# An attention, gating and mixing kernel on one core: key loads sent two blocks ahead, a limit of one side operation per engine and tick, and a normalisation on VectorE

## The chip, the cores and the metric

The kernel runs on one core of one Trainium2 chip. The metric is the device time of one execution in microseconds (us); lower is better. A profile is one execution taken by the hardware profiler: it lists the instructions of TensorE (PE, with its weight loads PEld), VectorE (DVE), ScalarE (ACT), GpSimd (POOL) and the DMA queue of SyncE (SP), each with its start and duration.

## What is computed

```python
def _attn_ref(q, k, v, n_global, n_local):          # (2, 8, 768, 64); 8 global keys, window 96
    scores = scale * np.matmul(q, k.transpose(0, 1, 3, 2)) + bias    # bias: -slope * distance
    scores = np.where(keep, scores, -1000000000.0)  # keep: global keys, or 0 <= rel < n_local
    a = softmax(scores)
    return np.matmul(a, v)

def _moe_ref(x, w_in, w_spatial, b_spatial, w_out): # x (2, 768, 512)
    h = np.maximum(x @ w_in, 0.0)                   # (2, 768, 1024)
    u, v = h[..., :512], h[..., 512:]
    v_n = (v - mean(v)) / np.sqrt(var(v) + 1e-06)
    v_s = np.einsum('ts,bsd->btd', w_spatial, v_n) + b_spatial[None, :, None]
    return (u * v_s) @ w_out

def _moe2_ref(x, U, V, w_ch1, w_ch2):
    u = x + (x.transpose(0, 2, 1) @ U @ V).transpose(0, 2, 1)
    return u + np.maximum(u @ w_ch1, 0.0) @ w_ch2
```

The three run one after the other. Weights come as 64-bit floats and are decoded on the chip.

## The kernel before

**Attention** runs over 12 blocks g (2 batches of 6 blocks of 128 queries), 8 heads in 4 pairs r, with 232 keys in a block's window (128 in the first block of a batch). In round g the emitted order is: scores of block g (`em_s`, 16 matmuls from the buffer `raw`, two buffers in turn), values of block g-2 (`em_pv`), softmax of block g (`em_soft` on DVE, `em_exp` on ACT, `em_norm` on DVE and POOL), and the transposes of block g-1 (`em_t`, four steps r, each copied out of PSUM to `ptb` by ACT or DVE). An engine runs its instructions in the order in which they were emitted.

**Side work** is emitted between these. It is kept as chains of operations (`Plan.add`); `Plan.tick` (line 160) walks through the chains and emits each next operation whose planned start lies close to TensorE's planned time, and repeats the walk until nothing more fits. `Plan.flush` emits what is left of given chains, at the place where their result is needed. The planned times come from prices in the code (`price`, line 105).

The side work of the attention stage is: the decoding of the first layer's `v` weights (`early_work`, line 667: four chains `P["wv"]`, each one ACT `Abs`, four DVE operations on 128x512, an ACT rounding and a POOL subtraction; places `rawin`, `masks`, `stg`), flushed before the first first-layer step; the spatial weights (`P["ws"]`, three chains: one DMA of 768 KB into one half of `stg`, then three ACT roundings and three subtractions, on POOL or DVE) and the spatial bias `P["bs"]`, flushed before the first spatial step; and `ln` (line 737), the reciprocal square root of the normalisation for three token tiles, followed by `ln_apply` for each tile (DVE scaling, ACT rounding, POOL subtraction into `vn`).

**Fillers** are matmul steps of the later layers put between the transposes by `fill(more)`: first-layer steps (`s_m1_v`, in rounds 4 to 9, 24 steps of batch 0), then spatial steps (`s_m2`, 48 steps of batch 0, from round 10 on). The spatial step with s == 3 flushes the second `ln` group of its batch. After the attention come the first layer of batch 1 (72 matmuls into `work`), the `u` half with its gating (`m1_u`, 8 steps, using `win`), the spatial product of batch 1, and then the output and mixing layers. `ln` of batch 1 belongs to the stretch of `m1_u`.

DMAs go out in order on SP's queue: `o_load` (keys and queries of a block), `o_vals` (values), and the weights.

Of the kernel before, what the change touches and what calls it, by code (L numbers as in the profile page):

```python
# [65 lines left out]
class Plan:  # L66
# [3 lines left out]
    def __init__(self, nc):  # L70
# [4 lines left out]
            ((nc.vector, "V"), (nc.scalar, "A"), (nc.gpsimd, "G"), (nc.tensor, "T"), (nc.sync, "SP")))  # L75
        self.chains = []

    @staticmethod
    def size(ap):
        n = 1  # L80
        for x in ap.shape[1:]:
            n *= x
        return n
# [63 lines left out]
                held[key][which, cols] = end  # L147
        return True

    def add(self, ops, after=()):  # L150
        c = Chain(ops, after, self.calm)
        self.chains.append(c)
        return c

    def emit(self, c):
# [2 lines left out]
            self.chains.remove(c)  # L158

    def tick(self):  # L160
        now, more = self.free["T"], True
        while more:
            more = False
            for c in sorted(self.chains, key=lambda c: c.calm):
                key = c.ops[0][0]
                if any(d.ops for d in c.after) or self.free[key] > now + (CALM if c.calm else ROOM):
                    continue
                self.probing = 0.0
                c.ops[0][1]()
                start, self.probing = self.probing, None  # L170
                if start <= max(now, self.free[key]) + STALL:
                    self.emit(c)
                    more = True

# [13 lines left out]
def kernel(ctx: ExitStack, tc: tile.TileContext, qk, qt, kn, vab, vn_, gl_,  # L188
# [11 lines left out]
    def body(dense, sb, pp):  # L200
# [142 lines left out]
        if not dense:  # L343
# [148 lines left out]
            def attention():  # L492
                for e in range(2):
                    o_load(0, e)[0][1]()
                o_vals(0)[0][1]()
                A.activation(out=sm[:, 12:13], in_=nc.const_aps.tensor(0.0, (128, 1)), func=AF.Exp)
                V.memset(bank[4], 0.0)
                V.memset(bank[7], 0.0)
                masks_before()
                make_identity(nc, ident)  # L500
                loads = {}
                for e in range(2):
                    o_load(1, e)[0][1]()
                pvals = {0: []}
                early_work([t_x11[:, 0:1536], t_x11[:, 1536:3072], t_x10[:, 1536:3072], stg[:, 0:1536]])
                pvals[1] = [plan.add(o_vals(1))]
                masks_first()
                masks_second()
                masks_third()
                for h in range(5, 8):  # L510
                    bias_g(Bt, rel, mk, h)


                for g in range(NBL + 2):
                    more = 0 if g < 4 else 1 if g < TWO else 3
                    if g == NB:
                        second_x()
                    xs = None
                    if g < NBL:
                        flush(loads.get(g, []))  # L520
                        for r in range(NP):
                            em_s(g, r)
                        if 0 < g and g + 1 < NBL:
                            loads[g + 1] = [plan.add(o_load(g + 1, e)) for e in range(2)]
                        tick()
                    if g >= 2:
                        flush(pvals[g - 2])
                        em_pv(g - 2)
                        if g < NBL:
                            pvals[g] = [plan.add(o_vals(g))]  # L530
                        xs = em_x(g - 2)
                    if g < NBL:
                        if g == 0:
                            for h in range(2, 4):
                                o_bias(B0, d0, m1, h)[1]()
                        em_soft(g, 0)
                        em_exp(g, 0)
                    if 0 < g <= NBL:
                        em_norm(g - 1, 1)
                    if g < NBL:  # L540
                        em_soft(g, 1)
                        em_exp(g, 1)
                        if g == 0:
                            for h in range(4, 8):
                                o_bias(B0, d0, m1, h)[1]()
                    if xs:
                        xs[0]()
                    for r in range(NP):
                        if xs and r == 1:
                            xs[1]()  # L550
                        if 0 < g <= NBL:
                            em_t(g - 1, r)
                            tick()
                        fill(more)
                        if g < NBL:
                            if r < 2:
                                em_soft(g, 2 + r)
                                em_exp(g, 2 + r)
                            if r == 1:
                                em_norm(g, 0)  # L560
                        tick()
                    if g == 0:
                        for h in range(5):
                            o_bias(Bt, rel, mk, h)[1]()
                        plan.add([("V", f) for f in o_counts() + o_flag()])
                    if 2 <= g < NB + 2:
                        fillers.extend(s_m1_v(0, g - 2, 6))
                    if g == TWO - 1:
                        fillers.extend(s_m2(0, 6))

# [96 lines left out]
        def early_work(places):  # L667
# [12 lines left out]
            u_ = tl(T_UT, N_UT, "u")  # L680
            P["ut"] = u_.rearrange("p (k t) -> p k t", k=KB)
            P["vw"] = [[u_[:, DM * n:DM * n + DM] for n in range(NB)]]
            P["bs"] = plan.add([o_dma(bsp, b_sp.partition_broadcast(128))], P["wv"][-1:])

            def make(t, c):
                return ([o_dma(t, w_sp.rearrange("p s t -> p (s t)")[:, c:c + 1536])]
# [49 lines left out]

        def ln(b, g):

            c = slice(3 * g, 3 * g + 3)
            e, q_, r = ve[:, b, c], rt[:, b, c], rs[:, b, c]  # L740

            def o_mult(o_, i0, i1):
                return "G", lambda: G.tensor_tensor(out=o_, in0=i0, in1=i1, op=ALU.mult)

            newton = [o_mult(q_, r, r), o_mult(q_, q_, e),
                      ("G", lambda: G.tensor_scalar(out=q_, in0=q_, scalar1=-0.5, scalar2=1.5, op0=ALU.mult, op1=ALU.add)),
                      o_mult(r, r, q_)]
            first = plan.add([
                ("V", lambda: V.tensor_scalar(out=e, in0=mv[:, b, c, 1], scalar1=1.0e-6, scalar2=None, op0=ALU.add)),
                ("V", lambda: V.tensor_scalar(out=r.bitcast(I32), in0=e.bitcast(I32), scalar1=1, scalar2=-1,  # L750
                                              op0=ALU.logical_shift_right, op1=ALU.bitwise_xor)),
                ("G", lambda: G.tensor_scalar(out=r, in0=r, scalar1=-1.8346686e-20, scalar2=0.0, op0=ALU.mult,
                                              op1=ALU.add))] + 3 * newton)
            return [plan.add(ln_apply(b, t), [first]) for t in range(3 * g, 3 * g + 3)]

        def ln_apply(b, t):
            vw = P["vw"][b][t]
            hi, lo = (P["vn"][b][l][:, t] for l in range(2))
            return [("V", lambda: V.tensor_scalar(out=vw, in0=vw, scalar1=mv[:, b, t, 0:1], scalar2=rs[:, b, t:t + 1],
                                                  op0=ALU.subtract, op1=ALU.mult)),  # L760
                    o_rnd(A, hi, vw), o_sub(G, lo, vw, hi)]

        def m1_u(b, f, j, bk):
            for k in range(KB):
# [273 lines left out]
```

## Time and profile before

| | us |
|---|---|
| median of 3 runs | 548.46 (546.75 to 548.96) |
| profiled execution, device time | 549.51 |
| its span, first to last instruction | 547.7 |
| PE busy | 513.8 |
| DVE / ACT / POOL busy | 299.7 / 212.0 / 196.6 |

All computing instructions carry line 56 (a recording helper), so groups are told apart by the names of what they write and read. Mean granted TensorE clock is 0.973 of full speed. PE is without a gap in most of the span; where it has gaps, the releaser beside an idle time names the instruction that came last before PE went on. A granted clock below 1 in a stretch is a share of the stretch in which TensorE ran at the lower of its two levels (1.2 GHz instead of 2.4).

### The profile page before, as it was taken

The numbers are of one execution on the slowest core, as the hardware profiler recorded it, in microseconds if no ns is written. First come the engines' busy times: TensorE is split into PE (matmuls) and PEld (weight loads), VectorE is DVE, ScalarE is ACT, GpSimd is POOL, SyncE is SP. The second block draws the span as 40 slices with busy tenths as digits, with TensorE's granted clock in tenths as the row PEclk, the third lists the DMA queues.
The fourth block names the chain that finished last, engine by engine and source line by source line (L and its number), as shares of the span: only waits on it lengthen the run. The fifth ranks groups of instructions, "written<-read, shape, count | busy, mean of one in ns | idle before, by whom it ended". The sixth has DMA issues, their size and how long they took to land.

```text
span 547.7 us, 7987 instructions
## 1 busy us (share of the span) xinstructions
PE 513.8 (94%) x2916; PEld 454.6 (83%) x2916; DVE 299.7 (55%) x702; ACT 212.0 (39%) x510; POOL 196.6 (36%) x265
## 2 busy tenths in 40 slices
PE   5579989699999899999999999999999999999994
PEld 3458868599989799888898989989989889899893
DVE  8886587343588963388699876866032011111113
ACT  4588768441244421355454234243122122221220
POOL 5466666621158801222024243232331332322310
PEclk9969989899999799999999999999999999999999
DMA  8617634130142110422204444240011000000003
GB/s 302 245 51 230 216 112 167 39 116 1 20 135 75 32 44 0 155 77 78 77 1 153 158 151 142 89 153 2 1 44 72 1 0 1 2 0 1 0 3 120
DMA packets 13521, 44.75 MB, mean 82 GB/s; under 512 B 1568, under 2 KB 3744, under 8 KB 11424
## 3 DMA queue, kind: packets, MB, share of 16 engines
q1 hardware_dynamic: 13328, 44.14, 23.1%
q8 instruction: 25, 0.41, 0.3%
q14 instruction: 24, 0.20, 0.1%
q10 hardware_dynamic: 144, 0.00, 0.0%
HBM read 40.99 MB, written 3.15 MB: 81 GB/s over the span
## 4 chain that ended last, share of the span: by engine, by line
PE 82%; DVE 7%; POOL 4%; ACT 4%; issue 2%; DMA 1%; ACTq 0%; POOLq 0%
PE bank L56 82%; DVE prob L56 2%; POOL sm L56 1%; ACT prob L56 1%; POOL vn L56 1%; DVE sm L56 1%; DVE y L56 1%; ACT ptb L56 1%; DVE stg L56 1%; DMA ni<-in_gl_dram 1%; DVE work L56 1%; DVE bias L56 1%; POOL wo L56 1%; POOL x L56 0%; DVE u L56 0%
## 5 line engine op out<-in xcount | busy, mean ns | idle before, releaser
L56 POOL TENSOR_TENSOR wch<-f,wch 128x512 fp32r<-128x512 f32 x64 | 86.1, 1366 | 213.3 <-ACT wch L56 213.3
L56 PE MATMUL bank<-wch,h 128*128 128x512 f32 x576 | 139.4, 396 | 0.0
L56 PE MATMUL bank<-x,wch 128*128 128x384 f32 x768 | 139.1, 337 | 0.0
L56 PEld LDWEIGHTS bank<-x,wch 128*128 128x128 f32 x768 | 134.5, 188 | 3.1
L56 PEld LDWEIGHTS bank<-wch,h 128*128 128x128 f32 x576 | 107.9, 188 | 23.2
L56 DVE SCALAR_TENSOR_TENSOR h<-bank,h 128x384 fp32r<-128x384 f32 x64 | 35.6, 556 | 141.5 <-ACT h L56 141.5
L56 ACT ACTIVATE h<-bank 128x384 fp32r<-128x384 f32 x64 | 31.4, 491 | 179.5 <-PE bank L56 179.5
L56 PE MATMUL bank<-wsp,vn 128*128 128x384 f32 x288 | 59.9, 362 | 7.0 <-POOL vn L56 5.0
L56 PEld LDWEIGHTS bank<-wsp,vn 128*128 128x128 f32 x288 | 53.0, 202 | 10.2 <-POOL vn L56 7.7
L56 POOL TENSOR_SCALAR prob<-prob,sm 128x232 f32<-128x232 f32 (+1 forms) x96 | 43.7, 473 | 40.8 <-DVE sm L56 19.8
L56 ACT ACTIVATE prob<-prob,sm 128x232 f32<-128x232 f32 (+1 forms) x96 | 44.4, 464 | 34.4 <-DVE sm L56 33.0
L56 DVE TENSOR_SCALAR f<-f 128x512 f32<-128x512 f32 (+1 forms) x64 | 41.4, 683 | 9.5 <-ACT f L56 9.3
L56 DVE SCALAR_TENSOR_TENSOR f<-raw,f 128x512 int32<-128x512 int32 x64 | 43.9, 726 | 0.1
L56 PE MATMUL bank<-win,x 128*128 128x512 f32 x144 | 40.1, 414 | 0.0
L56 PE MATMUL bank<-ident,prob 128*128 128x128 f32 (+1 forms) x176 | 29.6, 295 | 11.0 <-ACT ptb L56 10.9
L56 ACT ACTIVATE wch<-f 128x512 fp32r<-128x512 f32 x64 | 36.9, 625 | 1.0 <-DVE f L56 1.0
L56 PEld LDWEIGHTS bank<-ident,prob 128*128 128x128 f32 (+1 forms) x176 | 21.6, 144 | 18.6 <-POOL prob L56 10.5
L56 PE MATMUL bank<-x,win 128*128 128x384 f32 x192 | 34.2, 338 | 1.2 <-POOL win L56 0.7
L56 PE MATMUL bank<-wo,x 128*128 128x512 f32 x144 | 35.3, 395 | 0.0
L56 PEld LDWEIGHTS bank<-x,win 128*128 128x128 f32 x192 | 33.2, 188 | 2.0 <-POOL win L56 1.0
L56 PE MATMUL bank<-raw 64*128 64x232 f32 (+1 forms) x192 | 27.8, 436 | 7.5 <-DMA raw<-in_qk_dram 6.7
L56 PEld LDWEIGHTS bank<-raw 64*128 64x128 f32 x192 | 21.5, 238 | 12.8 <-DMA raw<-in_qk_dram 7.1
(85 smaller groups left out, 523.9 us busy)
## 6 DMA issues: line engine op xcount, KB each, us to landing
raw<-in_w_ch_dram SPq DMA_DIRECT2D x16, 1024.0 KB, 4.7
raw<-in_qk_dram SPq DMA_DIRECT2D x20, 360.0 KB, 4.8
vals<-in_vab_dram SPq DMA_DIRECT2D x10, 512.0 KB, 3.6
out_dram<-y SPq DMA_DIRECT2D x12, 256.0 KB, 2.2
stg<-in_w_in_dram SPq DMA_DIRECT2D x5, 512.0 KB, 5.0
stg<-in_w_sp_dram SPq DMA_DIRECT2D x3, 768.0 KB, 6.0
stg<-in_w_out_dram SPq DMA_DIRECT2D x4, 512.0 KB, 3.8
raw<-in_qk_dram SPq DMA_DIRECT2D x4, 256.0 KB, 5.0
```

The lines of the kernel that those rows point to most:

```text
L56: return f(*a, **kw)
```

## The change

- `o_load` for block g+2 is emitted directly after the scores of block g (before: as a chain for block g+1, added after the scores of block g and emitted by ticks). `o_vals` is emitted directly too. The `tick()` after the scores is gone.
- From the start of the attention to the end of round 11 a tick emits at most one side operation per engine (`plan.most = 1`).
- `ln` no longer uses POOL: for batch 0 the start value and three Newton steps of three operations run on DVE; for batch 1 an ACT `Sqrt`, a DVE `reciprocal` and one Newton step. Its chains and those of `ln_apply` are put in front of all others. The subtraction of the odd token tiles goes to DVE.
- The spatial bias waits until all four `v` weight chains are emitted, and the spatial chunk of the second staging half waits for it (before: that chunk could go at once).
- Round 10 runs one filler after each transpose instead of three, rounds from 11 on four.

```diff
-    def add(self, ops, after=()):
+    def add(self, ops, after=(), front=False):
         c = Chain(ops, after, self.calm)
-        self.chains.append(c)
+        self.chains.insert(0 if front else len(self.chains), c)
         return c
...
     def tick(self):
-        now, more = self.free["T"], True
+        now, more, count = self.free["T"], True, dict.fromkeys(LAG, 0)
...
+                if self.most and count[key] >= self.most:
+                    continue
                 self.probing = 0.0
                 c.ops[0][1]()
                 start, self.probing = self.probing, None
                 if start <= max(now, self.free[key]) + STALL:
+                    count[key] += 1
                     self.emit(c)
                     more = True
...
                 early_work([t_x11[:, 0:1536], t_x11[:, 1536:3072], t_x10[:, 1536:3072], stg[:, 0:1536]])
-                pvals[1] = [plan.add(o_vals(1))]
+                o_vals(1)[0][1]()
+                plan.most = 1
...
-                    more = 0 if g < 4 else 1 if g < TWO else 3
+                    more = 0 if g < 4 else 1 if g < TWO else 1 if g == TWO else 4
...
                     if g < NBL:
-                        flush(loads.get(g, []))
                         for r in range(NP):
                             em_s(g, r)
-                        if 0 < g and g + 1 < NBL:
-                            loads[g + 1] = [plan.add(o_load(g + 1, e)) for e in range(2)]
-                        tick()
+                        if g + 2 < NBL:
+                            for e in range(2):
+                                o_load(g + 2, e)[0][1]()
                     if g >= 2:
-                        flush(pvals[g - 2])
                         em_pv(g - 2)
                         if g < NBL:
-                            pvals[g] = [plan.add(o_vals(g))]
+                            o_vals(g)[0][1]()
                         xs = em_x(g - 2)
...
+                    if g == NBL - 1:
+                        plan.most = 0
...
-            P["bs"] = plan.add([o_dma(bsp, b_sp.partition_broadcast(128))], P["wv"][-1:])
+            P["bs"] = plan.add([o_dma(bsp, b_sp.partition_broadcast(128))], P["wv"])
+            user[1] = [P["bs"]]
...
-            newton = [o_mult(q_, r, r), o_mult(q_, q_, e),
-                      ("G", lambda: G.tensor_scalar(out=q_, in0=q_, scalar1=-0.5, scalar2=1.5, op0=ALU.mult, op1=ALU.add)),
-                      o_mult(r, r, q_)]
-            first = plan.add([
-                ("V", lambda: V.tensor_scalar(out=e, in0=mv[:, b, c, 1], scalar1=1.0e-6, scalar2=None, op0=ALU.add)),
-                ("V", lambda: V.tensor_scalar(out=r.bitcast(I32), in0=e.bitcast(I32), scalar1=1, scalar2=-1,
-                                              op0=ALU.logical_shift_right, op1=ALU.bitwise_xor)),
-                ("G", lambda: G.tensor_scalar(out=r, in0=r, scalar1=-1.8346686e-20, scalar2=0.0, op0=ALU.mult,
-                                              op1=ALU.add))] + 3 * newton)
-            return [plan.add(ln_apply(b, t), [first]) for t in range(3 * g, 3 * g + 3)]
+            newton = [stt(q_, r, -0.5, r, ALU.mult, ALU.mult),
+                      ("V", lambda: V.tensor_tensor(out=q_, in0=q_, in1=e, op=ALU.mult)),
+                      stt(r, q_, 1.5, r, ALU.add, ALU.mult)]
+            root = [("A", lambda: A.activation(out=q_, in_=e, func=AF.Sqrt)),
+                    ("V", lambda: V.reciprocal(out=r, in_=q_))]
+            bits = [o_ts(r.bitcast(I32), e.bitcast(I32), 1, -1, ALU.logical_shift_right, ALU.bitwise_xor),
+                    o_ts(r, r, -1.8346686e-20, None, ALU.mult)]
+            first = plan.add([o_ts(e, mv[:, b, c, 1], 1.0e-6, None, ALU.add)]
+                             + (root + newton if b else bits + 3 * newton), front=True)
+            return [plan.add(ln_apply(b, t), [first], True) for t in range(3 * g + 2, 3 * g - 1, -1)][::-1]
...
-                    o_rnd(A, hi, vw), o_sub(G, lo, vw, hi)]
+                    o_rnd(A, hi, vw), o_sub((G, V)[t % 2], lo, vw, hi)]
```

## Rows read from the trace of the kernel before

**Rows 1.** The page: PE's busy tenths and granted clock in 40 slices.
```profile
PE   5579989699999899999999999999999999999994
PEclk9969989899999799999999999999999999999999
```
**Rows 2.** Stretches: us, busy (instructions) of PE, PEld, DVE, ACT, POOL; clock; DMA share; GB/s.
```profile
17.00:45.00 28.00, 20.20 (x164) 16.28 (x165) 23.95 (x83) 18.91 (x58) 16.31 (x25) 0.82 0.39 139
70.00:79.00 9.00, 6.71 (x35) 4.69 (x35) 6.64 (x33) 5.60 (x20) 5.86 (x22) 0.81 0.37 142
100.00:113.00 13.00, 8.17 (x33) 6.40 (x33) 3.79 (x13) 3.20 (x8) 6.22 (x11) 0.74 0.00 1
160.00:174.00 14.00, 12.76 (x73) 12.12 (x72) 12.05 (x17) 4.95 (x9) 12.11 (x26) 1.00 0.26 75
181.00:190.00 9.00, 6.79 (x20) 5.35 (x20) 8.93 (x11) 4.55 (x9) 6.52 (x5) 0.64 0.12 34
```
**Rows 3.** PE in order of time: start us, us, what, count, [idle before <-releaser].
```profile
17.84 3.47 PE L56 MATMUL bank<-raw 64*128 64x232 f32 x16 [1.61 <-DMA raw<-in_qk_dram]
...
30.68 1.92 PE L56 MATMUL bank<-ident,prob 128*104 128x128 f32 x8 [6.47 <-ACT ptb L56]
...
40.92 1.84 PE L56 MATMUL bank<-raw 64*128 64x232 f32 x16
...
45.00 0.95 PE L56 MATMUL bank<-win,x 128*128 128x512 f32 x3
...
49.28 1.84 PE L56 MATMUL bank<-raw 64*128 64x232 f32 x16
...
106.72 3.14 PE L56 MATMUL bank<-wsp,vn 128*128 128x384 f32 x7 [3.75 <-POOL vn L56]
...
162.06 10.86 PE L56 MATMUL bank<-x,win 128*128 128x384 f32 x61 [0.66 <-POOL win L56]
...
183.74 25.27 PE L56 MATMUL bank<-wsp,vn 128*128 128x384 f32 x124 [1.25 <-POOL vn L56]
```
**Rows 4.** DVE in order of time, between the softmax of blocks 1 and 2.
```profile
17.73 0.99 DVE L56 TENSOR_SCALAR rawin<-rawin 128x512 f32<-128x512 f32 x2 [0.89 <-ACT rawin L56]
...
21.58 1.49 DVE L56 TENSOR_SCALAR masks<-masks 128x512 int32<-128x512 int32 x1
22.99 0.41 DVE L56 TENSOR_SCALAR stg<-stg 128x512 int32<-128x512 int32 x1
...
25.80 0.68 DVE L56 TENSOR_TENSOR wsp<-stg,wsp 128x512 fp32r<-128x512 f32 x1
...
27.07 0.39 DVE L56 CUSTOM_DVE_ANT_0 prob<-bank,bias 128x232 f32<-128x232 f32 x1
```
**Rows 5.** The SP queue's DMA issues in order of time.
```profile
6.17 0.51 SPq L56 DMA_DIRECT2D stg<-in_w_sp_dram  x1
...
7.61 4.91 SPq L56 DMA_DIRECT2D raw<-in_qk_dram  x4
...
59.92 0.33 SPq L56 DMA_DIRECT2D stg<-in_w_sp_dram  x1
```
**Rows 6.** ACT in order of time: the table load, and a spatial-weight rounding.
```profile
1.19 1.28 ACT L56 ACT_TABLE_LOAD   x1 [1.19 <-PEq L1025]
...
65.95 0.63 ACT L56 ACTIVATE wsp<-stg 128x512 fp32r<-128x512 f32 x1 [2.63 <-DMA stg<-in_w_sp_dram]
```
**Rows 7.** POOL in order of time, from 97 us on.
```profile
97.53 0.20 POOL L56 TENSOR_SCALAR sm<-sm 128x3 f32<-128x3 f32 x1
...
105.41 3.71 POOL L56 TENSOR_TENSOR vn<-u,vn 128x512 fp32r<-128x512 f32 x3
```
**Rows 8.** Groups by line, 150 to 195 us: count | busy us, mean ns | idle before.
```profile
L56 POOL TENSOR_TENSOR vn<-work,vn 128x512 fp32r<-128x512 f32 x6 | 8.6, 1468 | 0.0
...
L56 DVE TENSOR_SCALAR work<-work,sm 128x512 f32<-128x512 f32 x6 | 7.1, 1214 | 1.7 <-POOL sm L56 1.7
...
L56 DVE TENSOR_SCALAR sm<-sm 128x3 f32<-128x3 f32 (+1 forms) x4 | 1.4, 355 | 0.0
```

More of the change, by code (lines that the diff above doesn't have):

```diff
@@ L76, in __init__ @@
         self.chains = []
+        self.most = 0
     @staticmethod
@@ L500, in attention @@
                 make_identity(nc, ident)
-                loads = {}
                 for e in range(2):
                     o_load(1, e)[0][1]()
-                pvals = {0: []}
                 early_work([t_x11[:, 0:1536], t_x11[:, 1536:3072], t_x10[:, 1536:3072], stg[:, 0:1536]])
-                pvals[1] = [plan.add(o_vals(1))]
+                o_vals(1)[0][1]()
+                plan.most = 1
                 masks_first()
@@ L740, in ln, with stt, o_ts @@
             e, q_, r = ve[:, b, c], rt[:, b, c], rs[:, b, c]
-            def o_mult(o_, i0, i1):
-                return "G", lambda: G.tensor_tensor(out=o_, in0=i0, in1=i1, op=ALU.mult)
-            newton = [o_mult(q_, r, r), o_mult(q_, q_, e),
-                      ("G", lambda: G.tensor_scalar(out=q_, in0=q_, scalar1=-0.5, scalar2=1.5, op0=ALU.mult, op1=ALU.add)),
-                      o_mult(r, r, q_)]
-            first = plan.add([
-                ("V", lambda: V.tensor_scalar(out=e, in0=mv[:, b, c, 1], scalar1=1.0e-6, scalar2=None, op0=ALU.add)),
-                ("V", lambda: V.tensor_scalar(out=r.bitcast(I32), in0=e.bitcast(I32), scalar1=1, scalar2=-1,
-                                              op0=ALU.logical_shift_right, op1=ALU.bitwise_xor)),
-                ("G", lambda: G.tensor_scalar(out=r, in0=r, scalar1=-1.8346686e-20, scalar2=0.0, op0=ALU.mult,
-                                              op1=ALU.add))] + 3 * newton)
-            return [plan.add(ln_apply(b, t), [first]) for t in range(3 * g, 3 * g + 3)]
+            def stt(o_, i0, sc, i1, op0, op1):
+                return "V", lambda: V.scalar_tensor_tensor(out=o_, in0=i0, scalar=sc, in1=i1, op0=op0, op1=op1)
+            def o_ts(o_, i0, s1, s2, op0, op1=ALU.add):
+                return "V", lambda: V.tensor_scalar(out=o_, in0=i0, scalar1=s1, scalar2=s2, op0=op0,
+                                                    **({} if s2 is None else {"op1": op1}))
+            newton = [stt(q_, r, -0.5, r, ALU.mult, ALU.mult),
[8 more added lines that the diff above has]
+            return [plan.add(ln_apply(b, t), [first], True) for t in range(3 * g + 2, 3 * g - 1, -1)][::-1]
         def ln_apply(b, t):
```

## The prediction, made before the changed kernel was run

> **What bounds the kernel now.** I read first the page's slices: PE is nine tenths busy almost everywhere, and its holes and the lowered clock lie in the first 200 us of 548 [rows 1]. Only that part can change; from the third layer on PE runs without a hole until the last output. Second the table of stretches [rows 2], which I cut where PE has holes. In each, stretch minus PE busy is idle time, and (1 - clock) x stretch is what the lower clock (1.2 instead of 2.4 GHz) cost at most. Stage A, 17 to 45 us: 7.8 idle and 5.0 clock, 12.8. Stage B, 70 to 79: 2.3 and 1.7, 4.0. Stage C, 100 to 113: 4.8 and 3.4, 8.2. Stage D, 160 to 174 and 181 to 190: 1.2 + 2.2 idle and 3.2 clock, 6.7 with rounding. Together 31.7 us; apart from the start no edit can give more. Third, PE in order of time, which names who ended each hole [rows 3]: a key load (1.6 us before 17.84), a copy on ACT (6.5 before 30.68), the normalised tiles from POOL (3.75 before 106.72; 1.25 before 183.74). Fourth, the named engine's own order around each hole.
>
> **The change part by part.**
>
> *Stage A: key loads ahead, one side operation per tick, spatial chunk later.* Before the hole at 30.68 DVE ran one bulk of side work, from 17.73 until its softmax of block 2 began at 27.07: 9.3 us of decoding, small counts and one spatial subtraction [rows 4]. Softmax, ACT's exponentials and its copy stand behind this in order, so PE waited. With one operation per tick, and no tick behind the scores, the four chains' 16 DVE operations are spread over the ticks of rounds 2 and 3 (8 each). They stay in front of the same flush, so DVE's own work is not less. What does go: the spatial subtraction, 0.68 [rows 4], moves behind stage A with its ACT and POOL parts; and integer scalings that ran beside POOL's spatial subtractions took up to 1.49 against 0.41 without [rows 4]. Three stood there, at most 3.2 lost; I take 2.0. So DVE needs 23.95 - 2.7 = 21.3 us of a stage of 28.0 [rows 2], and the gain has 6.7 as its upper end. I take 4.5, leaving 2.2 of the 4.0 us that DVE idles there now, since softmax still waits for PE and ACT. The load of block 2 was issued behind a 768 KB spatial chunk (6.17, then 7.61 us, [rows 5]); that chunk now comes later and the load waits only for the scores of block 0. The 1.6 us before 17.84 go, but PE then meets the DVE bound, so they are not counted apart. The lower end is none gained, for the limit may leave operations over for the flush at the first filler (45.00, [rows 3]).
>
> The row of 1.49 against 0.41 is, by the Trainium skill (SBUF — State Buffer, Who interferes with whom), an exclusive lock of a port pair that VectorE and GpSimd share. By that rule the spatial chunk would carry its loss of 2.0 us into a later stage; there PE has fillers to run meanwhile, and the sum stays; without them it would be -13.0.
>
> *The direct loads add waits on SP*: a load for g+2 waits for the scores of block g, and values for the product of block g-2; behind them on SP stand the bias and the spatial chunks. Those are first used in round 10, and the last one was issued at 59.92 [rows 5], four rounds earlier, so I cost this at nothing; without that cover a chunk's 6.0 us from issue to use (59.92 to 65.95, [rows 5, 6]) would be bare.
>
> *Stage B.* Its hole of 2.3 us goes back to ACT: it stood 2.63 us at a spatial rounding whose DMA had not landed [rows 6], and the softmax of the next block stood behind. The change doesn't take this away: a rounding is still emitted when the plan believes the chunk there. Of two chunks issued late, one waited; now all three are late, and the limit lets only one rounding stand in a tick. Ends: -4.0 (no wait) and +4.0 (two waits of this price). I take 0, between them, since the one row speaks for either.
>
> *Stage C.* `ln` of tiles 3 to 5 ended the hole: its 13 small POOL operations began at 97.53, three DVE scalings and a softmax step followed, and POOL's three subtractions from 105.41 [rows 7]; PE went on at 106.72. After: 12 small DVE operations, which a DVE group on three elements puts at 0.36 [rows 8], at most 4.3 us, one per tick; the 16 ticks of round 10 hold them and the three scalings, and two of the subtractions go to DVE. Above all round 10 runs only 4 of the 12 spatial steps, so the first step that needs tile 3 falls in round 11, a round later: 8.4 us, as from 40.92 to 49.28 [rows 3]. All 8.2 us are the upper end; none is the lower. I take 6.0: small operations 4.3, scalings 3 x 0.41 and subtractions 2 x 0.68 [rows 4] put up to 6.9 us in front of round 10's softmax, where fewer fillers cover it, and I let a third of that, 2.2, come back.
>
> *Stage D.* POOL is full here, 12.1 of 14 us, and so is DVE, 8.9 of 9 [rows 2]. Batch 1's two `ln` groups cost POOL 26 small operations and six subtractions of 1.47 [rows 8]; three of these go to DVE, whose like (0.68, [rows 4]) is half as long. The chains stand in front: behind the last tile (162.06, [rows 3]) come five small operations (1.8), a table load, three scalings (3.6) and a subtraction (1.5), so `vn` should be ready near 171, before 183.74 - 1.25 = 182.5 where PE waits for it now. DVE's six scalings took 1.21 each beside POOL [rows 8], against 0.41 alone; with less on POOL some shorten. New: one `Sqrt` per group, hence a table load; the only one in the trace took 1.28 us [rows 6], and behind it on ACT stand copies of PSUM banks which PE reuses every fourth tile. That covers it, at nothing; without the cover 1.3 per group. And `ln` in front of the weights' decoding holds back the last `win` chunk, on which PE already waits 0.66 at 162.06 [rows 3]: about 2 us, one group's scalings and subtractions. Ends -6.7 and 0; I take -4.5.
>
> The Trainium skill (ScalarE: Activation LUTs, What ACT_TABLE_LOAD costs) puts a switch at 2.66 us with its drain. By that instead of the row the uncovered price would double, and the sum stays.
>
> **The sum.** -4.5 + 0 - 6.0 - 4.5 = -15.0. Against the profiled execution's 549.5 (span 547.7 and 1.8 around it) that gives 534.5; this execution lies 1.05 over the median 548.46, so I put the median at 533.5. All upper ends (-25.6) give 523; all lower ones (+4.0) 552.5, but they would have to meet.
>
> **The rivals.**
>
> *ACT waits in front of the chunks.* All three chunks land after their roundings are emitted, as at 65.95. Three waits at stage B's 4.0, less the one now: +8, so 541.5. For: one of two late ones did wait. Against: the first of those did not.
>
> *POOL and DVE as one resource.* If each waits for the other, small operations and subtractions moved to DVE lengthen its queue by what POOL saves: C halves to 3 (only the postponed steps help) and D falls to 1, with A -8.5 in all: 540. For: 1.21 against 0.41 for a scaling, in a stretch where both are full. Against: in stage C DVE has 3.8 busy of 13 [rows 2]. By the Trainium skill (Perfetto Trace Analysis, Optimizing Scalar/DVE Operations) moving work between these two might not help; this is that rule.
>
> *The limit doesn't do what it says.* If DVE's bulk only moves to the next ticks or into the flush, A is 0: 538.
>
> *Slower: the limit starves the decoding.* A tick takes a DVE operation only where DVE isn't ahead of TensorE in the plan. If nearly none is taken in rounds 1 to 3, the flush before the first filler emits all of it: 9.3 us of DVE, then four POOL subtractions of 1.24 [rows 7], 14.3 us bare. The scores of block 4 would come at 32.9 (two rounds of 8.4 after 17.84 - 1.61), and the first filler 4.1 (40.92 to 45.00) plus 14.3 later, at 51.3 instead of 45.00: +6.3, and some 3.4 of clock as in stage C. The same limit then leaves `ln` to its flush (C is 0), chunks wait (+4), D stays: +9.2, 558. It decides from where fewer than about half of the 16 operations are out by round 4. Against: the plan put nine microseconds of DVE work behind TensorE's time there, so it takes DVE as free.
>
> **How the numbers follow.** Forecast 0.60, ACT waits 0.13, one resource 0.07, limit without effect 0.07, starved 0.09, and 0.04 that two of the middle ones meet near 548. A difference of 0.5% (2.7 us) is about the least that a measurement of this kernel can tell from none. Faster by more than that: 0.60 + 0.27, less 0.03 for the upper tails of those cases, 0.84; within it: 0.04 + 0.03 = 0.07; slower 0.09. The range runs from 523, all upper ends, to 545, above which lie the starved case, the meeting ones and part of the tails.
>
> **What would show it.** Right: no hole over 3 us at PE between 17 and 45; DVE's decoding interleaved with softmax; the first filler near 40; no small POOL operations of `ln`, and no hole before the spatial steps of round 11; `vn` of batch 1 ready before PE comes to it. Wrong: PE waiting on `win` at the first filler, ACT roundings of `wsp` released by DMAs, a longer wait on `win` at 162, or a lowered clock in the same stretches.

## The result, and the profile after

The changed kernel takes **541.49 us** (median of 4 runs, 541.09 to 542.11) beside 548.71 for the kernel before (4 runs, 546.75 to 549.4): a ratio of 0.9875, 95% interval 0.9848 to 0.9902. That is 7.2 us, where 15 were forecast: inside the range (523 to 545), 8.0 above the forecast time. The time equals that of the rival "ACT waits in front of the chunks" (541.5), but by chance: in the changed kernel no rounding of `wsp` waits for its DMA. The page of the changed kernel, its span, PE, and the granted clock in 40 slices:

```profile
span 539.3 us, 7978 instructions
PE 506.0 (94%) x2916; PEld 447.9 (83%) x2916; DVE 305.6 (57%) x734; ACT 213.5 (40%) x513; POOL 176.0 (33%) x207
...
PEclk9886999999999999999999999999999999999999
```

The lowered clock is gone from the later stages and stands in slices 2 to 4, 13 to 54 us; before it was lowest in slice 3 [rows 1]. PE in order of time (columns as in [rows 3]) says why:

```profile
15.92 3.14 PE L56 MATMUL bank<-raw 64*128 64x232 f32 x16
...
42.07 0.80 PE L56 MATMUL bank<-win,x 128*128 128x512 f32 x1 [8.44 <-ACT win L56]
44.35 1.22 PE L56 MATMUL bank<-win,x 128*128 128x512 f32 x2 [1.49 <-POOL win L56]
...
80.71 0.62 PE L56 MATMUL bank<-ident,prob 128*104 128x128 f32 x4 [1.12 <-ACT ptb L56]
...
97.74 0.62 PE L56 MATMUL bank<-ident,prob 128*104 128x128 f32 x4 [1.13 <-ACT ptb L56]
99.71 0.62 PE L56 MATMUL bank<-ident,prob 128*104 128x128 f32 x4 [0.82 <-DVE sm L56]
101.63 0.65 PE L56 MATMUL bank<-ident,prob 128*104 128x128 f32 x4 [0.78 <-ACT ptb L56]
...
158.45 0.62 PE L56 MATMUL bank<-x,win 128*128 128x384 f32 x2 [1.34 <-ACT win L56]
159.91 15.01 PE L56 MATMUL bank<-x,win 128*128 128x384 f32 x85 [0.84 <-POOL win L56]
...
189.49 11.20 PE L56 MATMUL bank<-wsp,vn 128*128 128x384 f32 x63 [0.34 <-DVE u L56]
```

The key load is no longer waited for (15.92 against 17.84 [rows 3]). The hole before 30.68 is gone, but one of 8.44 us stands before the first filler, with 1.49 behind it. The holes before 106.72 and 183.74 are gone; smaller ones of 0.78 to 1.13 us stand before the transposes of round 10. Between 33 and 51 us the clock was 0.62 (stretch, columns as in [rows 2]):

```profile
33.00:51.00 18.00, 8.07 (x32) 5.88 (x32) 12.84 (x31) 9.34 (x23) 8.34 (x10) 0.62 0.43 134
```

To see where the time went, I cut both kernels at four marks on PE: the start of the scores of block 5, of block 10, of batch 1's first layer, and the end of that batch's spatial product. A is the first mark itself, B, C and D the distances between them (us).

| | A: to block 5 | B: to block 10 | C: to first layer | D: to end of spatial | sum |
|---|---|---|---|---|---|
| before | 49.28 | 43.66 | 50.02 | 66.05 | 209.01 |
| changed | 50.72 | 41.04 | 47.25 | 61.68 | 200.69 |
| difference | +1.44 | -2.62 | -2.77 | -4.37 | -8.32 |
| forecast | -4.5 | 0 | -6.0 | -4.5 | -15.0 |

The spans differ by 8.4, so nothing of size lies elsewhere. (These are two executions; the medians differ by 7.2.) D came as forecast. A went the wrong way, C brought half, and B brought what I had left at nothing. The same marks serve for every run below. A of one kernel can differ by about 1 us from execution to execution (48.17, 48.94 and 49.28 in three kernels with the old stage A), but in the seven kernels that decode as the changed one does it is 50.7 to 51.5, so that A is longer is clear.

Where the holes went, the clock came back. In B, C and D together PE's idle time fell by 3.2 us, but its busy time by 6.6 for the same matmuls, while the granted clock rose from 0.96, 0.93 and 0.95 to 1.00. In D 0.9 us of the 4.4 is idle time and 3.4 busy time.

### The profile page after: what moved, and what is told of

Its sections match the earlier page's. It is cut to its first block, busy times and chain, and to the rows that moved or that the text cites. A ratio compares the mean times of both kernels' runs of the same rounds, so it can differ in the third digit from the quotient of the medians.

```text
span 539.3 us, 7978 instructions
## 1 busy us (share of the span) xinstructions
PE 506.0 (94%) x2916; PEld 447.9 (83%) x2916; DVE 305.6 (57%) x734; ACT 213.5 (40%) x513; POOL 176.0 (33%) x207
## 4 chain that ended last, share of the span: by engine, by line
PE 79%; DVE 11%; ACT 5%; issue 2%; DMA 1%; POOL 1%; ACTq 0%; SPq 0%; DVEq 0%
PE bank L56 79%; DVE stg L56 3%; DVE sm L56 2%; DVE prob L56 1%; ACT prob L56 1%; DVE y L56 1%; ACT ptb L56 1%; DVE u L56 1%; DMA stg<-in_w_in_dram 1%; DVE vn L56 1%; DMA ni<-in_gl_dram 1%; ACT stg L56 1%; DVE bias L56 1%; DVE work L56 1%; ACT x L56 0%
## 5 line engine op out<-in xcount | busy, mean ns | idle before, releaser
L56 PE MATMUL bank<-wsp,vn 128*128 128x384 f32 x288 | 54.7, 341 | 1.1 <-POOL vn L56 0.3
L56 PEld LDWEIGHTS bank<-wsp,vn 128*128 128x128 f32 x288 | 49.2, 188 | 2.8 <-DVE u L56 0.9
L56 PE MATMUL bank<-win,x 128*128 128x512 f32 x144 | 41.4, 422 | 9.9 <-ACT win L56 8.4
L56 PEld LDWEIGHTS bank<-win,x 128*128 128x128 f32 x144 | 26.3, 197 | 14.6 <-ACT win L56 8.7
L56 DVE CUSTOM_DVE_ANT_0 prob<-bank,bias 128x232 f32<-128x232 f32 (+1 forms) x96 | 31.7, 369 | 2.6 <-PE bank L56 2.6
```

Source lines behind the costliest of these rows:

```text
L56: return f(*a, **kw)
```

## Experiments on stage A: why did the decoding come late?

ACT in order of time in the changed kernel, then DVE, at the hole before 42.07:

```profile
34.22 1.21 ACT L56 ACTIVATE rawin<-rawin 128x512 f32<-128x512 f32 x2
...
34.91 0.98 DVE L56 TENSOR_SCALAR rawin<-rawin 128x512 f32<-128x512 f32 x2 [2.49 <-ACT rawin L56]
...
42.47 0.68 DVE L56 SCALAR_TENSOR_TENSOR stg<-stg 128x512 int32<-128x512 int32 x1
```

All 16 decoding operations run in one piece, 34.91 to 43.1, in the flush before the first filler: the place that my "slower" rival named. Each chain begins with ACT's `Abs`, which ran here at 34.22, and in the kernel before at 17.05 (its ACT row):

```profile
17.05 1.21 ACT L56 ACTIVATE rawin<-rawin 128x512 f32<-128x512 f32 x2
```

There are two theories: the `tick()` behind the scores, which the change removed, was the place where the `Abs` went out; or the limit holds the chains back.

**e1_tick**: the tick put back, the limit kept.

```diff
                             for e in range(2):
                                 o_load(g + 2, e)[0][1]()
+                        tick()
```

> The changed kernel with the tick after the scores put back; the limit of one operation per engine and tick stays. Theory (no tick after the scores is left in which ACT isn't ahead of TensorE in the plan, so the decoding's first operation, ACT's Abs, never goes out before the flush): in rounds 2 and 3 two of the four chains get out, the hole before the first filler falls from 8.4 us to about 4, and the time to 537 to 540 from 541.5. Rival (the limit itself starves the decoding): the limit stands as before, the hole stays over 7 us and the time within 541 to 542.

Measured: 539.0 us, ratio 0.9827 [0.9789, 0.9865]; A 46.25, 4.5 less than in the changed kernel. Two `Abs` go out at 17.15 and 25.30, one per round; the other two chains still come in the flush, and PE waits for them in small pieces:

```profile
37.43 0.51 PE L56 MATMUL bank<-win,x 128*128 128x512 f32 x1 [1.26 <-ACT win L56]
38.86 0.73 PE L56 MATMUL bank<-win,x 128*128 128x512 f32 x2 [0.93 <-POOL win L56]
41.61 0.75 PE L56 MATMUL bank<-win,x 128*128 128x512 f32 x1 [1.58 <-ACT win L56]
42.97 1.22 PE L56 MATMUL bank<-win,x 128*128 128x512 f32 x2 [0.60 <-POOL win L56]
```

So the missing tick was what held the chains back: with it two of the four start in time.

**e2_nolimit**: the changed kernel with `plan.most = 0` instead of 1.

> The changed kernel without the limit of one operation per engine and tick (all else as changed). Theory (the missing tick, not the limit): the decoding still stands in one piece before the first filler, the hole there stays at 8 to 9 us, and stage A is as in the changed kernel; later rounds can differ, with the old hole near 73 us back if the limit was what took it away: 541 to 545. Rival (the limit starves): the hole at the first filler goes and the time falls to 534 to 537.

Measured: 550.18 us, ratio 1.0051 [1.0031, 1.0071]. The hole at the first filler is the same, so the limit had no part in it. But three holes come back (the last three lines):

```profile
43.26 0.79 PE L56 MATMUL bank<-win,x 128*128 128x512 f32 x1 [8.44 <-ACT win L56]
...
76.94 0.66 PE L56 MATMUL bank<-ident,prob 128*128 128x128 f32 x2 [3.26 <-DVE ptb L56]
102.24 0.62 PE L56 MATMUL bank<-ident,prob 128*104 128x128 f32 x4 [0.95 <-POOL prob L56]
107.00 1.07 PE L56 MATMUL bank<-ident,prob 128*104 128x128 f32 x4 [3.61 <-DVE ptb L56]
```

B is 45.50 and C 50.16: in this kernel the limit is worth 4.5 and 2.9 us there.

**e3_spread**: the chains put out by hand, two in round 2 and two in round 3, an operation per engine at each of the eight places of a round.

```diff
                             em_t(g - 1, r)
+                            spread(g)
                             tick()
```

> The changed kernel with the four decoding chains emitted by hand, two in round 2 and two in round 3, one operation per engine at each of the eight places of a round. Theory (placing is all that failed in stage A): no hole over 2 us at the first filler, which starts at 36 to 40 instead of 42.1, scores of block 5 at 44 to 46 instead of 50.7, time 535 to 537. Rival (DVE's work is the bound wherever it stands): rounds 2 and 3 lengthen by what the hole gives back, scores of block 5 at 49 to 50, time 540 to 542.

Measured: 541.7 us, ratio 0.9896 [0.9869, 0.9923]; A 49.23. These are the rival's numbers, but its reason isn't shown, for DVE was busy 22.96 of the 30 us from 17 to 47. The waits moved: a DVE operation put out right behind its `Abs` waited until ACT had done the exponentials in front of it, and DVE's copy of the transposes stood behind (DVE, then PE):

```profile
22.91 0.43 DVE L56 TENSOR_SCALAR rawin<-rawin 128x512 f32<-128x512 f32 x1 [3.06 <-ACT rawin L56]
...
25.66 0.62 PE L56 MATMUL bank<-ident,prob 128*104 128x128 f32 x4 [2.58 <-DVE ptb L56]
```

**e8_spread2**: the same by hand from the second half of round 1, and never in the same place as the operation of another engine that it waits for.

```diff
+    if key in used or (where == place[0] and last != key):
+        continue
```

> The changed kernel with the four decoding chains put out by hand from the second half of round 1 to the end of round 3, one operation per engine and place, and none in the same place as the operation of another engine that it waits for. Theory 1 (the decoding only needs an earlier place, and time between an operation and its producer): the hole of 8.4 us at the first filler goes, no hole over 1.5 us takes its place in rounds 2 and 3, the scores of block 5 start at 44 to 46 instead of 50.7, and the time is 535 to 537. Theory 2 (DVE's work bounds the stage): the holes only move in front of the transposes of rounds 2 and 3, the scores of block 5 start at 48 to 51 and the time is 539 to 542.

Measured: 538.09 us, ratio 0.9828 [0.9798, 0.9858]; A 46.80, between the two expectations. With e15 and e16 (further down) this is the lowest median, and the three lie within 0.3 us. No wait for `win` is left, but there are holes at the transposes (1.65, 1.51 and 3.08 us). The stretch shows DVE 28.12 of 30.00 us busy:

```profile
17.00:47.00 30.00, 23.37 (x188) 18.61 (x188) 28.12 (x91) 21.39 (x66) 18.55 (x28) 0.89 0.59 191
```

In this order DVE has hardly any room left. It isn't the bound of every order, though: e1, with two chains in the flush, had A 46.25 with DVE busy 25.08 us of the same stretch. **e12_spread1** began half a round earlier still.

> The changed kernel with the four decoding chains put out by hand as in the run that spread them from the second half of round 1 (538.1 us), but from the first half of round 1. Theory 1 (the earlier the decoding, the less stands beside the softmax of rounds 2 and 3): the scores of block 5 start before 46.8 us, at 45 to 46, time 536.5 to 537.5. Theory 2 (DVE's work from 14 to 44 us is the same, and it has no gap before 34 us but the two us at 15.7): the holes only move, scores of block 5 at 46.5 to 48.5, time 538 to 539.5.

Measured: 539.18 us, ratio 0.984 [0.9811, 0.987], A 46.53: the second expectation, no further gain. In the three kernels where an earlier decoding helped, A is 46.25 to 46.80 (e1, e12, e8), on average 2.3 below the three old ones, where I had forecast 4.5. No run has the direct loads alone: e14 and e16 below, with the tick and the limit but the old loads and the old place of the chunk, have A 47.24 and 47.44, 1.0 to 1.2 above e1, about the scatter.

**e6_chunk_early**: the first spatial chunk and the bias sent as before (`P["bs"]` waits for `P["wv"][-1:]`, `user[1]` not set).

> The changed kernel with the first spatial chunk and the bias sent as before, not behind the decoding of the first layer's weights. The hole of 2.3 us near 73 is gone in the changed kernel, and ACT waited for no chunk. Theory 1: the limit of one operation per tick took it away, the place of the chunks did not: no hole over 1.5 us between 65 and 80, time 541.5 within 1.5. Theory 2: the later chunk took it away, since ACT's rounding is emitted when its data is there: ACT stands at a rounding of `wsp` again, the hole of about 2.3 us comes back and the time is 544. In the decoding stage the early chunk's POOL subtractions stand beside DVE's integer scalings again: if these cost the 2.0 us that I forecast, the scores of block 5 start at 52 to 53 instead of 50.7, else at 50.7.

Measured: 541.84 us, ratio 0.9882 [0.9852, 0.9911]; A 51.15, B 41.06. The hole of stage B doesn't come back, so it was the limit that removed it (e2, and e14 below). For A the run doesn't test what it was meant to: the chunk was sent at 12.66, but its first rounding still stands at 45.06, behind the decoding (43.73 in the changed kernel), so POOL's subtractions don't meet the scalings in either kernel. The 2.0 us that I took off DVE for them did come: the four integer scalings took 1.6 us in the changed kernel (36.92 to 38.34) and 3.7 before (19.83 to 23.40). They were worth nothing to PE there, since the decoding stood in the flush.

## Experiments on stages C and D: which part brought what?

**e4_fill3** is the changed kernel with `more = 3` from round 10 on, as before.

> The changed kernel with three spatial steps per transpose from round 10 on, as before the change. Theory (postponing the steps is what removed the hole before the second group of tiles; the DVE version of ln isn't ready in round 10 either): a hole of 3 to 5 us in round 10 and 543 to 546. Rival (ln on DVE suffices, and the postponed steps only starve PE in round 10): no hole over 1.5 us there, the 2.7 us by which round 10 is longer than its matmuls go, and 538.5 to 541.

Measured: 544.97 us, ratio 0.9956 [0.9944, 0.9969], C 49.44: in this kernel the postponed steps are worth 2.2 us of C, and the time is the first theory's.

**e5_ln_pool** is the changed kernel with the old `ln` and `ln_apply`.

> The changed kernel with `ln` and `ln_apply` as they were before (small steps of the root on POOL, all `vn` subtractions on POOL, at the end of the list). Theory 1: the gain at the start of batch 1's second layer (the second layer's end came 4.4 us nearer to its start) is all from `ln`, and in round 10 `ln` on DVE costs nothing; then the time from the start of batch 1's first layer (139.0 in the changed kernel) to the end of its second layer (200.5) goes from 61.5 back to 65.9 us, round 10 stays at 11.0 us, and the time is about 546. Theory 2: in round 10 the moved small steps lengthen DVE's queue in front of the softmax; then round 10 falls from 11.0 to near 9 us while the second layer gives its 4.4 back: about 544. Rival (VectorE and GpSimd as one resource): moving `ln` is worth nothing in either place: 541.5, and both stretches stay.

Measured: 551.67 us, ratio 1.0073 [1.0048, 1.0098], slower than before the change. C is 53.57 and D 66.13: here `ln` is worth 6.3 us in C, which no theory had so high, and 4.5 in D. PE in this kernel:

```profile
98.38 0.45 PE L56 MATMUL bank<-wsp,vn 128*128 128x384 f32 x1 [2.72 <-POOL vn L56]
...
112.33 0.62 PE L56 MATMUL bank<-wsp,vn 128*128 128x384 f32 x2 [3.21 <-ACT vn L56]
```

**e11_ln_only** asks the same from the other side: the kernel before with nothing but the new `ln` and `ln_apply`.

> The kernel before with the new `ln` and `ln_apply` alone (first in the list of chains, root on DVE, half of the subtractions on DVE). Taking `ln` out of the changed kernel cost 10.2 us. Theory 1 (the parts add): alone it brings as much, about 538: hole at 106.72 gone (3 to 4 us), 4.5 us in batch 1's second layer, the rest in rounds 10 and 11. Theory 2 (in batch 0 it needs the postponed spatial steps and the limit to be worth anything): only the 4.5 us of the second layer, and at most 1.5 of the hole at 106.72: 542 to 545.

Measured: 540.45 us, ratio 0.988 [0.9846, 0.9913], between the two theories. The whole change is not faster than this part of it. C is 44.51, the lowest of all kernels, and D 62.39. DVE, then PE:

```profile
95.54 1.01 DVE L56 TENSOR_SCALAR sm<-sm 128x3 f32<-128x3 f32 x3
...
98.59 1.46 DVE L56 TENSOR_SCALAR u<-u,sm 128x512 f32<-128x512 f32 x3
99.97 0.68 DVE L56 TENSOR_TENSOR vn<-u,vn 128x512 fp32r<-128x512 f32 x1
...
102.63 0.62 PE L56 MATMUL bank<-ident,prob 128*104 128x128 f32 x4 [2.27 <-DVE ptb L56]
```

The 12 small steps took 95.54 to 98.59, 3.05 us, and the first `vn` subtraction began at 99.97, where POOL began its three at 105.41 before [rows 7]. One hole of 2.27 us is left of 1.09 and 3.75.

Measured from the scores of block 10 the first subtraction begins 5.0 us earlier. Of these 2.0 are the small steps: before, two on DVE from 96.02 and 13 on POOL, to 101.06, took 5.0 with the hand-over. The other 2.9 are order: the subtraction now follows DVE's scalings at once, while before POOL had the softmax's scalings of `prob` in front of its three, and waited there for ACT (POOL in the kernel before):

```profile
103.69 1.76 POOL L56 TENSOR_SCALAR prob<-prob,sm 128x232 f32<-128x232 f32 x4 [2.62 <-ACT prob L56]
```

This edit moves `ln` to another engine, puts its chains first and gives half of the subtractions to DVE; no run separates the three.

**e13_fill_only** is the kernel before with the new numbers of fillers alone.

> The kernel before with 1 spatial step per tick place in round 10 and 4 in round 11, instead of 3 and 3, and nothing else. Theory 1 (my forecast for that stage: the first step that needs tile 3 falls a round later, and by then the tile is there): the hole of 3.75 us before 106.72 goes, at most 2.2 us come back as holes in round 10, and the time is 544 to 546.5. Theory 2 (`ln` runs on the small POOL steps and its flush stands as late as before): the steps that ran in round 10 now stand in round 11, and a hole of 3 us or more stays at the first step that needs the next tiles: 547.5 to 550.

Measured: 546.16 us, ratio 0.996 [0.9936, 0.9984], C 48.07: the postponed steps do take away the wait for `vn`, as the first theory has it, and holes of 0.59, 0.42 and 2.64 us in round 10 come in its place.

**e14_limit_only** is the kernel before with the limit alone.

> The kernel before with the limit of one side operation per engine and tick, from after the early loads to block 11, and nothing else (the tick behind the scores stays). Taking the limit out of the changed kernel cost 8.7 us. Theory 1 (the limit helps by itself: no bulk of decoding before the hole at 30.68, no bulk behind the softmax of rounds 8 and 10): hole at 30.68 under 3 us, hole at 73 gone, time 541 to 544. Theory 2 (with POOL's long `ln` chain a limit only makes the chains later): holes at the first step of round 10 or 11 that needs new tiles grow by what the others lose, time 547 to 551.

Measured: 548.24 us, ratio 1.0007 [0.9987, 1.0027]: no difference, as a sum of three (in one execution each): A 47.24 (-2.0), B 41.16 (-2.5), C 52.83 (+2.8):

```profile
95.00 0.79 PE L56 MATMUL bank<-wsp,vn 128*128 128x384 f32 x3 [1.40 <-POOL vn L56]
...
103.67 1.01 PE L56 MATMUL bank<-wsp,vn 128*128 128x384 f32 x2 [2.96 <-ACT vn L56]
```

With these runs stage C is known for every mixture of three parts (us, start of block 10's scores to batch 1's first layer). They stand on two bases: those marked * have the loads, the tick and the chunk of the kernel before, the others those of the changed kernel.

| | 3 fillers, no limit | 3 fillers, limit | 1 filler, no limit | 1 filler, limit |
|---|---|---|---|---|
| old `ln` | 50.0* (before) | 52.8* (e14) | 48.1* (e13) | 53.6 (e5) |
| new `ln` | **44.5*** (e11) | 49.4 (e4) | 50.2 (e2) | 47.3 (changed) |

The best is the new `ln` alone. Only cells of one base differ by one part: added to the kernel before, `ln` gives 5.5, the postponed steps give about 2 and the limit costs 2.8; taken out of the changed kernel, `ln` costs 6.3, the limit 2.9 and the postponed steps 2.2. So the limit is a loss alone and a gain in the changed kernel. Between the bases the base counts too: e16 and e17 below have the same three parts, and C 46.5 and 47.3. And in e2, not in e11, side work held back until then stands in round 10: POOL had a `vn` and a `wsp` subtraction there, and two small DVE steps beside them took 2.44 us:

```profile
102.18 2.44 DVE L56 SCALAR_TENSOR_TENSOR sm<-sm 128x3 f32<-128x3 f32 x2
```

What the limit or the postponed steps would cost beside the new `ln` on the base of the kernel before is therefore not shown.

**e17_free10** and **e16_ln_limit10** try to have the limit's gain in A and B without its loss in C. The first is the changed kernel, the second the kernel before with the new `ln` and the limit; both end the limit after round 9 and run 3 fillers.

```diff
-                    if g == NBL - 1:
+                    if g == TWO - 1:
                         plan.most = 0
```

> The changed kernel with the limit lifted from round 10 on (instead of block 11) and 3 spatial steps per tick place in rounds 10 and 11, as before the change. From the start of block 10's scores to batch 1's first layer the kernel before took 50.0 us, the changed one 47.3, the kernel before with the new `ln` alone 44.5. Theory 1 (the limit holds back `ln` in round 10, and the postponed steps only mend that): this stretch falls to 44.5 to 45.5 us, and the time is 538.5 to 540. Theory 2 (what helped there was the room that the kernel before had gained by its later rounds, with the side work out earlier): lifting the limit lets a bulk of held-back work out in front of round 10's softmax, the stretch takes 47 to 50 us, and the time is 541.5 to 544.

Measured: 541.98 us, ratio 0.9891 [0.9869, 0.9913], C 47.31: the second theory. Side work held back until then stands in round 10. On POOL it is a `vn` subtraction of a tile of the first group, for which PE and a DVE step wait (POOL, DVE, PE):

```profile
97.92 1.27 POOL L56 TENSOR_TENSOR vn<-u,vn 128x512 fp32r<-128x512 f32 x1
...
98.00 1.21 DVE L56 TENSOR_TENSOR sm<-sm 128x3 f32<-128x3 f32 x1
...
99.24 0.45 PE L56 MATMUL bank<-wsp,vn 128*128 128x384 f32 x1 [0.93 <-POOL vn L56]
```

> The kernel before with the new `ln` and the limit from the early loads up to round 10, the ticks behind the scores and all else as before. By stages: with the limit alone the scores of block 10 started at 88.4 (92.9 before); with `ln` alone the stretch from there to batch 1's first layer took 44.5 (50.0 before) and from there to the end of its second layer 62.4 (66.1 before). Theory 1 (the stages add): 88.4 + 44.5 + 62.4 = 195.3 at the end of that layer, against 209.0 before and 200.7 in the changed kernel, so about 535.5. Theory 2 (the limit leaves work over that comes out in front of round 10's softmax): that stretch takes 47 us or more, and the time is 538 to 541.

Measured: 538.37 us, ratio 0.983 [0.9811, 0.9849]; A 47.44, B 42.25, C 46.45, D 61.63. The time is at the lower end of the second theory, C between the two: two parts of the change, with the limit ended earlier, beat all of them by about 3 us. **e15_spread_free10** puts e17's edit on e8.

> The changed kernel with the decoding put out by hand from the second half of round 1 (538.1 us alone) and the limit lifted from round 10 on with 3 steps in rounds 10 and 11. If the two places are independent, this is 538.1 plus what lifting the limit brings beside it: theory 1 -2.0 to -3.0, 535.5; theory 2 0 to +2.5, 538 to 540.5.

Measured: 538.28 us, ratio 0.9824 [0.9799, 0.9848], C 46.27, D 62.53 (e8: 47.24 and 61.64): nothing more than e8.

**e10_sub_dve** is the changed kernel with all `vn` subtractions of batch 0 on DVE (`V if b == 0 or t % 2 else G`).

> The changed kernel with all `vn` subtractions of batch 0 on DVE (one of three per `ln` group or two stand on POOL in the changed kernel). In the changed kernel a DVE step on three elements took 1.12 us at 97.24, while POOL ran a `vn` subtraction of 1.27 us from 97.07, and 0.13 to 0.15 elsewhere. Theory 1 (a DVE instruction with two inputs waits for a POOL instruction that runs): without that POOL subtraction the step at its place takes under 0.2 us, round 10 is 0.5 to 1.3 us shorter than 11.0, and the time is 540.5. Rival (the step's own cost, or its producer): it stays near 1.1 us, DVE gets 0.7 us more work per subtraction, and the time is 541.5 to 542.5.

Measured: 541.78 us, ratio 0.9895 [0.9865, 0.9925], C 46.97. The small DVE step at that place fell from 1.12 to 0.31 us, most of the way that the first theory has it, but the time stayed, as the rival has it. The holes before the transposes of round 10 are 1.73, 0.41 and 0.88 us there, 3.0 against 2.7, so another wait took what the step gave back; each subtraction also costs DVE 0.68. Whether the step was on the path is not shown.

## Why the prediction was wrong in size

**A (forecast -4.5, came +1.4).** The step that failed is "the four chains' 16 DVE operations are spread over the ticks of rounds 2 and 3". I named the removed tick as a help, and didn't ask which operation begins a chain: ACT's `Abs`, for which only the removed tick had a place (e1). The rival "the limit starves the decoding" had the mechanism, a flush before the first filler, with another cause and too high a price: I gave it 14.3 us bare, it was 8.44 + 1.49, and rounds 2 and 3, free of decoding, took 7.0 and 6.4 us (scores at 15.92, 22.89 and 29.30) instead of 8.4, so the first filler came at 42.07, not 51.3. The second error is the size: even with the decoding placed earlier, the gain is about 2.3 (e1, e8, e12). My 21.3 us of DVE work left out that scalings and POOL's subtractions meet again when the chains are spread: in e8 a scaling of `stg` took 1.50 us at 30.30, while POOL ran a `win` subtraction from 29.81 to 31.52, and the same scaling of `rawin` 0.43 at 17.80.

**B (0, came -2.6).** Inside its bounds. The term asked when chunks land; the limit decided it instead (B is 39.8 to 42.6 us in the thirteen kernels with the limit, 43.5 to 45.5 in the four without), and sending the first chunk early changed nothing (e6).

**C (-6.0, came -2.8).** The step that failed is "Above all round 10 runs only 4 of the 12 spatial steps". I put the gain on the postponed steps and took the moved small steps for a loss to be covered. It is the other way round: the new `ln` alone gives -5.5 (e11), near the forecast sum by chance, since the first `vn` subtraction begins five us earlier and one hole of 2.27 is left. And the postponed steps postponed `ln` too. The flush that completes it stands in front of the first step that needs tile 3, so it fell a round later with that step. I had the 16 ticks of round 10 hold the small steps and the scalings; only 6 of the 12 steps ran before the scores of block 11 (102.73). From the first step to the last it was 11.3 us here, against 3 in e11 (DVE, then POOL in the changed kernel):

```profile
95.69 1.01 DVE L56 TENSOR_SCALAR sm<-sm 128x3 f32<-128x3 f32 x3
...
106.84 0.16 DVE L56 SCALAR_TENSOR_TENSOR sm<-sm 128x3 f32<-128x3 f32 x1
107.04 1.46 DVE L56 TENSOR_SCALAR u<-u,sm 128x512 f32<-128x512 f32 x3
...
108.87 1.36 POOL L56 TENSOR_TENSOR vn<-u,vn 128x512 fp32r<-128x512 f32 x1 [2.08 <-ACT vn L56]
```

With three fillers under the same limit it was 5.6 us (e4), with one filler and no limit 10.6 (e2), so this delay is the postponed steps' more than the limit's. What I had let come back, 2.2, was 2.73 in the three holes of round 10, with three more waits of 0.2 to 0.4 us in round 11.

**D (-4.5, came -4.4).** Right in its sum and its cause (e5 gives 4.5 back), by its steps only in part. `vn` was ready at 171.62 (forecast "near 171"), but the stage began 4 us earlier, so that is 4.6 later within it: the second group's small steps took 157.65 to 164.58, where I had 1.8 us, and the last two subtractions on DVE 3.18, where I had each at half of POOL's 1.47. It was still there before PE's spatial product began (174.75). The holes of 0.76 and 1.25 us before 181.88 and 183.74 are gone, and with them the lowered clock of 181 to 190 [rows 2], which is most of the gain; and the last `win` chunk is waited for longer, 1.34 + 0.84 against 0.66 (forecast "about 2 us"). The table load is there once, and ACT lost no more than its row (ACT in order of time):

```profile
148.33 0.67 ACT L56 ACTIVATE stg<-stg 128x512 f32<-128x512 f32 x1 [0.31 <-DMA stg<-in_w_in_dram]
149.01 1.28 ACT L56 ACT_TABLE_LOAD   x1
150.30 0.21 ACT L56 ACTIVATE sm<-sm 128x3 f32<-128x3 f32 x1
```

The Trainium skill (ScalarE: Activation LUTs, What ACT_TABLE_LOAD costs) puts such a switch at 2.66 us, about half of it a drain. This trace shows the load's 1.28 and the `Sqrt` 0.01 us behind it, so here the row decides.

**What stays open.** Why e15 and e16 keep C at 46.3 to 46.5 and not at 44.5 is shown only in part. Both have a hole of 2.3 to 2.7 us for DVE's `ptb` copy, as e11 has. Beside it e15 waits 0.93 for a leftover `vn` subtraction on POOL, and e16's PE is busy 43.79 us at a clock of 0.96, against 42.24 at 1.00 in e11; no run removes the leftover alone. Nor do the holes account for all of the changed kernel's C: PE was busy 8.23 + 35.37 us in it (up to and from block 11's scores), against 12.04 + 30.20 in e11 for the same matmuls, 1.4 us more at the full clock in both. Some 0.8 of this is that the first 12 spatial matmuls of round 11 ran in four pieces between holes, 3.14 us in sum, where the next 12, in one piece, took 2.33. And no run tells which of the new `ln`'s three edits gives its gain.

## What to carry to other kernels

Before a tick, a flush or any other place of emission is removed, list what begins at that place, by the first engine of each chain, not by the engine that does most of its work. A term for one stage that rests on three edits has to be priced for the edits alone and together: the limit lengthened stage C by 2.8 us alone and shortened it by 2.9 in the changed kernel. Before a step is postponed, ask what is emitted in front of it: what it waits for may be postponed with it. And a small hole can cost more than its length: in D the holes that went were 2 us, and PE's busy time fell by 3.4 as the clock came back.

## What was new about the hardware

A DVE step on three elements with two inputs, 0.13 to 0.17 us long with POOL idle, took 1.12 to 1.26 us where POOL ran 128x512 subtractions of 1.27 to 1.47 (97.24 and 161.51 in the changed kernel, 98.00 in e17), and ended 0.02 to 0.03 us behind POOL's each time. Not the work but the neighbour set its time; in e10, with POOL's scalings of `prob` in its place, the step took 0.31. By the Trainium skill (SBUF — State Buffer, Who interferes with whom) a VectorE instruction with two inputs from this memory contends with GpSimd's reads; the traces agree. The prediction had priced the small steps at 0.36.
